# Three x tiles turned by DMA instead of TensorE, and the beginnings of blocks 1 and 2 cut differently, in a fused cosformer attention and GEGLU block

## The chip, the cores and the metric

The kernel runs on one core of a Trainium2 chip. A core has five engines that take their instructions in order and work side by side: TensorE (PE in the profile, with its weight loads as PEld), VectorE (DVE), ScalarE (ACT), GpSimd (POOL) and SyncE (SP), which here only issues DMAs. The metric is the device time of one execution in microseconds (us), as the median of several.

## The reference

Linear attention with a cosine weighting, then a gated feed-forward block:

```python
# q, k, v: 8 batches, 8 heads, 576 positions, 64 wide
def phi(x, c, s):
    r = np.maximum(x, 0.0)
    return np.concatenate([r * c, r * s], axis=-1)      # c, s: cos and sin of pi/2 * pos/576
q_p, k_p = phi(q, cos_w, sin_w), phi(k, cos_w, sin_w)
kv = np.einsum('bhsf,bhsd->bhfd', k_p, v)
z = np.sum(k_p, axis=2)
num = np.einsum('bhsf,bhfd->bhsd', q_p, kv)
den = np.einsum('bhsf,bhf->bhs', q_p, z)[..., None] + 1e-06
attn = num / den
# x: 4608 tokens of 512; w_gate, w_val: 512 x 1536; w_out: 1536 x 512
out = (gelu(x @ w_gate) * (x @ w_val)) @ w_out
```

The output is 4608 x 512 in float32.

## The kernel before

**Attention, batch by batch.** q, k and v of a batch (name `qf`, `kf`, `vf` in the profile) are loaded in two halves each. `prep` makes phi: the cosine half on VectorE (L162), the sine half on ScalarE (L160), a slice of positions `j` at a time; a 256-column instruction each. `kv_unit(b)` (L241) makes kv and z on TensorE. q's phi must be turned so that features lie on partitions: for batches 0 and 1 TensorE does it (`turn_j`, L204), from batch 2 on `turn_q(b)` (L193) does it with two DMA transposes that SyncE issues. `nm_unit(b, t)` multiplies 128 turned positions by kv: eight matmuls of 65 columns (L282), then three VectorE instructions that divide by the denominator (L293, L294, L295) and leave an x tile, 128 tokens x 512. A batch of 576 positions has five x tiles, t = 0 to 4, the last with 64 new rows.

**Turning x.** The feed-forward block needs x with its 512 features on partitions. `turn_x(b, t)` (L349) does it by DMA transposes on SyncE's queue. `turn_x_pe` (L357) does it by four TensorE transposes into PSUM and a ScalarE copy (L361) out of it, two copies where the tile straddles two blocks. The result goes into `xT` of a block.

**Feed-forward, block by block.** The 4608 tokens are nine blocks of 512 columns (`BLK`). Batch boundaries fall inside blocks: block 1 holds x tile 4 of batch 0 (columns 0 to 63), then tiles 0, 1, 2 of batch 1 (from columns 64, 192 and 320) and the left 64 columns of its tile 3; block 2 begins with the rest of tile 3 and tile 4 of batch 1, 64 columns each, and then has tiles 0, 1, 2 of batch 2. `gv_unit(n, jt)` makes one of twelve units of gate and value: eight matmuls over the block's columns (L400), a GELU on ScalarE (L408), a product on VectorE (L409) into `hT`. Units use two pairs of PSUM banks in turn, so a unit waits for the product of the unit before the last. `o_part` multiplies `hT` by w_out (L430), twelve matmuls per 128 tokens, and ScalarE copies the sum to `o_sb` (L439). The output products of block n - 1 are done in thirds, one after each unit of block n; those of block 0 stand by themselves, between blocks 0 and 1.

**Starting a block before all of it is there.** The first units of blocks 1, 2 and 3 are done in two halves: first the left columns of several units, then the right columns of the same units. Before the change block 1 does so with two units, block 2 with four and block 3 with two, all split 256 + 256.

**What sets the order.** The schedule is manual: every engine executes its instructions in the order in which the Python program issues them, and only semaphores tie the engines together. Between blocks 0 and 1 a list named `order` sets the sequence (entries "o" for a third of an output product, "nm" for an x tile's matmuls, "xt" for an x tile turned by TensorE, "q2" for phi of q of batch 2). In blocks 1 to 8 the loop over `jt` puts attention work of the next batch between units; `t_kv`, `t_nm`, `t_q` and `t_k` say at which `jt`. SyncE's queue takes, in order, loads, q and x transposes, and the output stores; a DMA that waits for its source holds up all that stand behind it. `store` puts out one tile in two DMAs, `flush` all that are held in `stores`; `o_part` flushes the tile before it. GpSimd's queue has the weights and q, k, v of batches 1 and 2. The pools `qT`, `qp` and `kp` have one buffer each, so the next batch's turn of q waits until the last x tile of the batch before has read `qT`.

Of the kernel before, what the change touches and what calls it, by code (L numbers as in the profile page):

```python
# [16 lines left out]
def kernel(  # L17
# [13 lines left out]
    nc = tc.nc  # L31
# [6 lines left out]
    JT = J // 128  # L38
    NP = H // 2
    R = S // 64  # L40
# [3 lines left out]
    BLK = 512  # L44
    JA = 4
# [376 lines left out]
    def flush():  # L422
        for i, o_sb in stores:
            store((nc.sync, nc.sync), i, o_sb)
        stores.clear()

    def o_part(i, jts, to, copy):
        n, tt = divmod(i, 4)
        for jt in jts:
            nc.tensor.matmul(  # L430
                bank(to),
                lhsT=hT[n][:, jt, tt * 128:(tt + 1) * 128],
                rhs=wo_sb[:, jt, :],
                start=(jt == 0),
                stop=(jt == JT - 1),
            )
        if JT - 1 in jts:
            o_sb = outp.tile([128, C], FP32, name="o_sb")
            copy(o_sb, bank(to))  # L439
            flush()  # L440
            stores.append((i, o_sb))


# [28 lines left out]
    for m in (0, 2):  # L472
        load(nc.gpsimd, "v", 1, m, m + 2)
    load_wo(8, 4)
    for name in ("q", "k"):
        for m in (0, 2):
            load(nc.gpsimd, name, 2, m, m + 2)
    for m in (0, 2):
        load(nc.gpsimd, "v", 2, m, m + 2)

    def turn_j(b, m0, m1, js, to, copy):

# [55 lines left out]
    for jt in range(4, JT):  # L538
        gv_unit(0, jt)
        if jt == 5:  # L540
            turn_j(0, 0, 4, (R - 1,), 4, act_copy)
        if jt == 6:
            nm_unit(0, 4)
        if jt == 8:
            turn_x_pe(0, 4, 5, act_copy)
        if jt in q1:
            prep("q", 1, 0, q1[jt])
            prep("q", 1, 1, q1[jt], eng=nc.scalar)
# [10 lines left out]
    )  # L559
    for what, *a in order:  # L560
        if what == "o":
# [17 lines left out]
            nm_unit(1, a[0], a[1])  # L579
        if what == "xt":  # L580
            turn_x_pe(1, a[0], a[1], act_copy)
    for m in (0, 2):
        load(nc.sync, "q", 3, m, m + 2)


    def prep_third(name, b, i):
# [4 lines left out]
    def loads(b, names=("q", "k", "v")):  # L591
# [5 lines left out]


    q3 = {
        (1, 8): ((0,), (0, 1)),  # L600
        (1, 9): ((1,), (2, 3)),
        (1, 10): ((2,), (4, 5)),
        (1, 11): ((3, 4, 5), (6, 7)),
        (2, 0): ((6, 7), (8,)),
        (2, 1): ((8,), ()),
    }
    turn[0] = 1
    for n in range(1, NB):
        b = n + 1
        t_kv, t_nm, t_q, t_k = {1: (7, 9, 12, 12), 2: (6, 7, 7, 9), 3: (2, 5, 6, 9)}.get(  # L610
            n, (1, 2, 4, 8)
        )
        for jt in range(JT):
            if n == 1 and jt >= t_nm:
                nm_unit(2, jt - t_nm, (6, 4, 6)[jt - t_nm])
                turn_x(2, jt - t_nm)
            heads = (0, 2, 4, 2)[n] if n < 4 else 0
            if jt >= heads:
                gv_unit(n, jt)
            else:  # L620
                for i in range(2):
                    half, unit = divmod(2 * jt + i, heads)
                    gv_unit(n, unit, half * HALF, HALF)
                    if n == 1:
                        j = JA + 2 * jt + i
                        prep("q", b, 1, (j,), eng=nc.scalar)
                        prep("q", b, 0, (j,))
                        if jt == i == 0:
                            turn_x_pe(1, 3, 5, act_copy)
            if jt % 3 == 1:  # L630
                flush()
            if b < B:
                if n == 1 and jt == 2:
                    prep("q", b, 0, (R - 1,))
                    prep("q", b, 1, (R - 1,), eng=nc.scalar)
                    turn_q(b)
                    nm_unit(1, NT - 1)
                if n == 1 and jt == 3:
                    turn_x(1, NT - 1)
# [12 lines left out]
                if jt == t_kv:  # L652
                    kv_unit(b)
                i = jt - 1 - n if n <= 2 else -1
                if 0 <= i < 3:
                    prep_third("k", b, i)
# [12 lines left out]
                if n > 1 and b + 1 < B:  # L669
                    if 0 <= jt - t_q < 3:  # L670
                        prep_third("q", b + 1, jt - t_q)
                    if 0 <= jt - t_k < 3:
                        prep_third("k", b + 1, jt - t_k)
                for c, t in nms:
                    if t == NT - 1:
                        if c + 1 < B:
                            turn_q(c + 1)
                        if c + 2 < B:
                            loads(c + 2)
                        for i in range(-(-(BLK - 64 * c) // 128), NT):  # L680
                            turn_x(c, i)
            if n > 1:
                o_part(
                    4 * (n - 1) + jt // 3,
                    range(4 * (jt % 3), 4 * (jt % 3) + 4),
                    4,
                    act_copy,
                )
# [47 lines left out]
```

## Time and profile before

| | |
|---|---|
| median of 4 runs | 326.78 us (325.28 to 328.07) |
| the profiled execution's own time | 326.69 us |
| its span, first to last instruction | 324.7 us |
| TensorE busy | 317.0 us, 2451 matmuls |
| VectorE busy | 170.3 us, 407 instructions |
| ScalarE busy | 159.2 us, 336 instructions |
| GpSimd busy | 26.0 us, all of it in the first 45 us |
| HBM read, written | 37.75 MB, 9.44 MB |
| granted TensorE clock | 1.0 |

The profile is of one execution. Its busy times are unions of instruction times; matmuls overlap, so the distance between the starts of two matmuls is what one costs, and the printed length of one (379 ns for 512 columns) is longer. For VectorE and ScalarE too, the next instruction can start before the printed end. A line number is that of the function that issues an instruction, so one line stands for many places; the start times tell them apart. "us to landing" of a DMA counts from the start of its issue to the event that tells of its end.

### The profile page before, as it was taken

The numbers are of one execution on the slowest core, as the hardware profiler recorded it, in microseconds if no ns is written. First come the engines' busy times: TensorE is split into PE (matmuls) and PEld (weight loads), VectorE is DVE, ScalarE is ACT, GpSimd is POOL, SyncE is SP. The second block draws the span as 40 slices with busy tenths as digits, with TensorE's granted clock in tenths as the row PEclk, the third lists the DMA queues.
The fourth block names the chain that finished last, engine by engine and source line by source line (L and its number), as shares of the span: only waits on it lengthen the run. The fifth ranks groups of instructions, "written<-read, shape, count | busy, mean of one in ns | idle before, by whom it ended". The sixth has DMA issues, their size and how long they took to land.

```text
span 324.7 us, 6340 instructions
## 1 busy us (share of the span) xinstructions
PE 317.0 (98%) x2451; PEld 164.5 (51%) x2451; DVE 170.3 (52%) x407; ACT 159.2 (49%) x336; POOL 26.0 (8%) x43
## 2 busy tenths in 40 slices
PE   8799999999999999999999999999999999999995
PEld 3574556556745564545544554445544444444443
DVE  5854686759675952793585348544532222222211
ACT  7854767947365833674457336643222332222220
POOL 5775410000000000000000000000000000000000
PEclk9999999999999999999999999999999999999999
DMA  7999999952999889828956991543431111111124
GB/s 271 233 191 267 294 346 374 217 139 48 308 196 380 164 157 380 203 75 240 323 119 152 356 236 28 131 100 81 88 72 33 35 32 32 35 32 32 34 65 98
DMA packets 69102, 53.57 MB, mean 165 GB/s; under 512 B 45392, under 2 KB 54352, under 8 KB 69072
## 3 DMA queue, kind: packets, MB, share of 16 engines
q1 hardware_dynamic: 59264, 41.23, 48.8%
q0 software_dynamic: 9648, 11.80, 15.7%
q8 instruction: 19, 0.31, 0.4%
q10 hardware_dynamic: 160, 0.13, 0.1%
q14 instruction: 11, 0.09, 0.1%
HBM read 37.75 MB, written 9.44 MB: 145 GB/s over the span
## 4 chain that ended last, share of the span: by engine, by line
PE 93%; DMA 4%; POOL 1%; DVE 0%; SPq 0%; issue 0%; DVEq 0%
PE ps L400 56%; PE ps L430 28%; PE ps L282 3%; PE ps L241 3%; DMA vf<-in_v_dram 2%; DMA wv_sb<-in_moe_w_val_dram 2%; PE ps L697 1%; PE ps L372 1%; PE ps L204 1%; PE ps L357 0%; SPq L80 0%; POOL wg_sb L94 0%; POOL gate L458 0%; DVE x_sb L295 0%; DVE o_sb L704 0%
## 5 line engine op out<-in xcount | busy, mean ns | idle before, releaser
L409 DVE TENSOR_TENSOR hT<-gel,ps 128x512 bf16<-128x512 f32 (+1 forms) x114 | 74.0, 650 | 128.8 <-PE ps L400 125.8
L408 ACT ACTIVATE gel<-ps 128x512 f32<-128x512 f32 (+1 forms) x114 | 64.8, 568 | 109.7 <-PE ps L400 108.0
L400 PE MATMUL ps<-xT,wg_sb 128*128 128x512 bf16 (+1 forms) x456 | 110.2, 364 | 0.0
L400 PE MATMUL ps<-xT,wv_sb 128*128 128x512 bf16 (+1 forms) x456 | 110.2, 364 | 0.0
L430 PE MATMUL ps<-wo_sb,hT 128*128 128x512 bf16 x420 | 105.8, 379 | 0.0
L400 PEld LDWEIGHTS <-wv_sb 128*128 128x128 bf16 x456 | 44.6, 98 | 47.0
L400 PEld LDWEIGHTS <-wg_sb 128*128 128x128 bf16 x456 | 44.0, 98 | 46.1
L430 PEld LDWEIGHTS <-hT 128*128 128x128 bf16 x420 | 38.3, 98 | 39.4
L439 ACT COPY o_sb<-ps 128x512 f32<-128x512 f32 x34 | 19.9, 586 | 30.0 <-PE ps L430 28.7
L160 ACT ACTIVATE qp<-qf,sin_t 128x256 bf16<-128x256 f32 x72 | 32.0, 501 | 0.4 <-DMA qf<-in_q_dram 0.4
L160 ACT ACTIVATE kp<-kf,sin_t 128x256 bf16<-128x256 f32 (+1 forms) x73 | 29.9, 480 | 1.2 <-DMA kf<-in_k_dram 1.2
L295 DVE TENSOR_TENSOR x_sb<-ps,rec 128x512 bf16<-128x512 f32 x38 | 26.3, 692 | 1.3
L162 DVE TENSOR_SCALAR qp<-qf,cos_t 128x256 bf16<-128x256 f32 x71 | 22.0, 357 | 2.3 <-DMA qf<-in_q_dram 2.3
L282 PEld LDWEIGHTS <-qT 128*128 128x128 bf16 x304 | 14.6, 98 | 7.9 <-ACT qT L486 0.3
L162 DVE TENSOR_SCALAR kp<-kf,cos_t 128x256 bf16<-128x256 f32 x63 | 18.2, 349 | 0.0
L282 PE MATMUL ps<-kv_sb,qT 128*128 128x65 bf16 x304 | 16.0, 194 | 0.0
L179 DVE CAST vx<-vf 128x1152 bf16<-128x1152 f32 (+1 forms) x15 | 11.9, 800 | 0.8 <-DMA vf<-in_v_dram 0.7
L250 ACT CAST kv_sb<-ps 128x260 bf16<-128x260 f32 x14 | 4.6, 382 | 12.9 <-PE ps L241 12.9
L241 PEld LDWEIGHTS <-kp 64*128 64x128 bf16 x504 | 8.5, 95 | 3.0 <-issue 3.0
L140 PE MATMUL ps<-dummy 128*128 128x512 bf16 x27 | 8.4, 457 | 1.5 <-POOL dummy L113 1.5
L241 PE MATMUL ps<-vx,kp 64*128 64x65 bf16 x504 | 9.3, 191 | 0.0
L294 DVE RECIPROCAL rec<-den 128x8 f32<-128x8 f32 x38 | 7.7, 203 | 1.3
(60 smaller groups left out, 100.6 us busy)
## 6 DMA issues: line engine op xcount, KB each, us to landing
out_dram<-o_sb SPq DMA_DIRECT2D x70, 128.0 KB, 2.7
kf<-in_k_dram SPq DMA_DIRECT2D x12, 576.0 KB, 6.5
vf<-in_v_dram SPq DMA_DIRECT2D x12, 576.0 KB, 8.6
qf<-in_q_dram SPq DMA_DIRECT2D x10, 576.0 KB, 5.0
qf<-in_q_dram POOLq DMA_DIRECT2D x4, 576.0 KB, 12.1
kf<-in_k_dram POOLq DMA_DIRECT2D x4, 576.0 KB, 12.6
vf<-in_v_dram POOLq DMA_DIRECT2D x4, 576.0 KB, 12.7
wg_sb<-in_moe_w_gate_dram POOLq DMA_DIRECT2D x6, 256.0 KB, 6.7
```

The source lines that it names most:

```text
L140: nc.tensor.matmul(bank(to), lhsT=dummy[:, 0:128], rhs=dummy, start=True, stop=True)
L160: nc.scalar.activation(o, i, AF.Relu, scale=tab[:, j:j + 1])
L162: (eng or nc.vector).tensor_scalar(o, i, 0.0, tab[:, j:j + 1], op0=ALU.max, op1=ALU.mult)
L179: copy(vx_tiles[b % 2][:, m0:m1, j0:j1, 0:D], staged["v", b][:, m0:m1, j0 * D:j1 * D].rearrange("p m (j d) -> p m j d", d=D),)
L241: nc.tensor.matmul(bank(6 + i)[:, m * (D + 1):(m + 1) * (D + 1)], lhsT=kp[rr, m, j, :], rhs=vx[rr, m, j, :], start=(j == 0), stop=(j == R ...
L282: nc.tensor.matmul(bank(b0 + h // 4)[:, (h % 4) * (D + 1):(h % 4 + 1) * (D + 1)], lhsT=q_cols(b, t, h), rhs=kv_sb[b][:, h // 2, h % 2, :], ...
L295: nc.vector.tensor_tensor(x, nm[:, :, :, 0:D], rec[:, :, :, None].to_broadcast([128, 2, 4, D]), op=ALU.mult,)
L400: nc.tensor.matmul(bank(b0 + g)[:, 0:w], lhsT=wt[:, ct, js], rhs=xt[:, ct, c0:c0 + w], start=(ct == 0), stop=(ct == CT - 1),)
L408: nc.scalar.activation(gel[:, 0:w], bank(b0)[:, 0:w], AF.Gelu)
L409: nc.vector.tensor_mul(hT[n][:, jt, c0:c0 + w], gel[:, 0:w], bank(b0 + 1)[:, 0:w])
L430: nc.tensor.matmul(bank(to), lhsT=hT[n][:, jt, tt * 128:(tt + 1) * 128], rhs=wo_sb[:, jt, :], start=(jt == 0), stop=(jt == JT - 1),)
L439: copy(o_sb, bank(to))
```

## The change

- Tile 4 of batch 0 is turned by `turn_x` instead of `turn_x_pe`, at the same place.
- Tiles 2 and 3 of batch 1 are turned by `turn_x` (a new entry "xd" in `order`), right after their `nm_unit`; before, TensorE turned tile 2 at the end of `order` and tile 3 inside block 1's first step.
- The load of q of batch 3 moves from SyncE's queue, behind block 0, to the end of GpSimd's queue, behind v of batch 2.
- Block 0's four output tiles are stored together in block 1's fourth step, instead of one by one as they are made.
- Block 1 does six units in halves of 256 instead of two; block 2 does six units as 128 + 384 columns instead of four as 256 + 256. Block 3 is as before.
- phi of q and k of batch 2 goes between the half units of block 1, `turn_q(2)` is issued one step earlier, tiles 0 and 1 of batch 2 one step later (steps 10 and 11), tile 2 moves into block 2's first step and tiles 3 and 4 into its second and third. In those three steps the output thirds stand between the two narrow pieces of a step instead of after them.
- The loads of k and v of batch 3 are issued in block 2's first step, behind the turn of tile 2 of batch 2, instead of in block 1's last. phi of q of batch 3 is spread otherwise over the same steps, and phi of k of batch 2 starts earlier.

The diff, cut to what the text speaks of:

```diff
@@ o_part
             copy(o_sb, bank(to))
-            flush()
+            if n > 0:
+                flush()
             stores.append((i, o_sb))
@@ GpSimd's loads
-    for name in ("q", "k"):
+    for name, b in (("q", 2), ("k", 2), ("v", 2), ("q", 3)):
         for m in (0, 2):
-            load(nc.gpsimd, name, 2, m, m + 2)
-    for m in (0, 2):
-        load(nc.gpsimd, "v", 2, m, m + 2)
+            load(nc.gpsimd, name, b, m, m + 2)
@@ block 0
         if jt == 8:
-            turn_x_pe(0, 4, 5, act_copy)
+            turn_x(0, 4)
@@ order
-        + [("nm", 0, 2), ("o", 0, 8), ("nm", 1, 6), ("o", 1, 8), ("xt", 0, 4), ("nm", 2, 2)]
-        + [("q2", 2, 3), ("o", 2, 8), ("xt", 1, 5), ("nm", 3, 6), ("q2", 3, 4), ("o", 3, 8)]
-        + [("xt", 2, 4)]
+        + [("nm", 0, 2), ("o", 0, 8), ("nm", 1, 6), ("o", 1, 8), ("xt", 0, 4), ("nm", 2, 2), ("xd", 2)]
+        + [("q2", 2, 3), ("o", 2, 8), ("xt", 1, 5), ("nm", 3, 6), ("xd", 3), ("q2", 3, 4), ("o", 3, 8)]
...
-    for m in (0, 2):
-        load(nc.sync, "q", 3, m, m + 2)
+        if what == "xd":
+            turn_x(1, a[0])
@@ blocks 1 to 8
+    heads = {1: (6, HALF), 2: (6, 128), 3: (2, HALF)}
...
-        t_kv, t_nm, t_q, t_k = {1: (7, 9, 12, 12), 2: (6, 7, 7, 9), 3: (2, 5, 6, 9)}.get(
+        t_kv, t_nm, t_q, t_k = {1: (7, 10, 12, 12), 2: (6, 7, 7, 9), 3: (2, 5, 6, 9)}.get(
...
-            heads = (0, 2, 4, 2)[n] if n < 4 else 0
-            if jt >= heads:
+            h, mid = heads.get(n, (0, 0))
+            if jt >= h:
                 gv_unit(n, jt)
             else:
                 for i in range(2):
-                    half, unit = divmod(2 * jt + i, heads)
-                    gv_unit(n, unit, half * HALF, HALF)
-                    if n == 1:
-                        j = JA + 2 * jt + i
-                        prep("q", b, 1, (j,), eng=nc.scalar)
-                        prep("q", b, 0, (j,))
-                        if jt == i == 0:
-                            turn_x_pe(1, 3, 5, act_copy)
-            if jt % 3 == 1:
+                    half, unit = divmod(2 * jt + i, h)
+                    gv_unit(n, unit, *((mid, BLK - mid) if half else (0, mid)))
+                    if n == 1 and jt < 2:
+                        js = ((4,), (5,), (6,), (7, 8))[2 * jt + i]
+                        prep("q", b, 1, js, eng=nc.scalar)
+                        prep("q", b, 0, js)
+                    if n == 2 and jt < 3 and i == 0:
+                        o_third(n, jt)
+                    if n == 1 and jt > 1:
+                        j = 2 * jt - 4 + i
+                        prep("k", b, 0, (j,))
+                        prep("k", b, 1, (j,), eng=nc.scalar)
+            if jt % 3 == 1 and n > 1:
                 flush()
...
+                if n == 1 and jt == 1:
+                    turn_q(b)
                 if n == 1 and jt == 2:
-                    prep("q", b, 0, (R - 1,))
-                    prep("q", b, 1, (R - 1,), eng=nc.scalar)
-                    turn_q(b)
                     nm_unit(1, NT - 1)
                 if n == 1 and jt == 3:
                     turn_x(1, NT - 1)
+                    flush()
...
-                if n == 2 and jt < 2:
-                    nms.append((n, 3 + jt))
+                if n == 2 and jt < 3:
+                    nms.append((n, 2 + jt))
...
-                if n == 1 and jt == JT - 1:
-                    loads(3, ("k", "v"))
                 for bt in nms:
                     nm_unit(*bt)
+                if (n, jt) == (2, 0):
+                    turn_x(2, 2)
+                    loads(3, ("k", "v"))
```

`o_third(n, jt)` is the third of an output product that the loop had at its end.

More of the change, by code (lines that the diff above doesn't have):

```diff
@@ L599, with o_third @@
     q3 = {
[L600 to L605, printed above, removed]
-    }
+        (1, 9): ((0, 1, 2), (0, 1)),
+        (1, 10): ((), (2, 3)),
+        (1, 11): ((), (4, 5)),
+        (2, 0): ((3, 4), (6,)),
+        (2, 1): ((5, 6), (7,)),
+        (2, 2): ((7, 8), (8,)),
+    }
+    heads = {1: (6, HALF), 2: (6, 128), 3: (2, HALF)}
+    def o_third(n, jt):
+        o_part(
+            4 * (n - 1) + jt // 3,
+            range(4 * (jt % 3), 4 * (jt % 3) + 4),
+            4,
+            act_copy,
+        )
     turn[0] = 1
@@ L614 @@
             if n == 1 and jt >= t_nm:
-                nm_unit(2, jt - t_nm, (6, 4, 6)[jt - t_nm])
+                nm_unit(2, jt - t_nm, (6, 4)[jt - t_nm])
                 turn_x(2, jt - t_nm)
-            heads = (0, 2, 4, 2)[n] if n < 4 else 0
-            if jt >= heads:
+            h, mid = heads.get(n, (0, 0))
+            if jt >= h:
                 gv_unit(n, jt)
@@ L647 @@
                     turn_x(b, i)
-                if n == 1 and jt == JT - 1:
-                    loads(3, ("k", "v"))
                 for bt in nms:
                     nm_unit(*bt)
+                if (n, jt) == (2, 0):
+                    turn_x(2, 2)
+                    loads(3, ("k", "v"))
                 if jt == t_kv:
                     kv_unit(b)
-                i = jt - 1 - n if n <= 2 else -1
-                if 0 <= i < 3:
-                    prep_third("k", b, i)
+                if n == 1 and jt == 6:
+                    prep("k", b, 0, (R - 1,))
+                    prep("k", b, 1, (R - 1,), eng=nc.scalar)
+                if n == 2 and 3 <= jt < 6:
+                    prep_third("k", b, jt - 3)
                 i = 2 * (jt - 5) if n == 1 else jt - (4 if n == 2 else 0)
@@ L681 @@
                             turn_x(c, i)
[L682 to L688, printed above, removed]
+            if n > 2 or n == 2 and jt > 2:
+                o_third(n, jt)
     for t in range(3):
```

## The prediction

> **What bounds the kernel now.** I read the page first (busy shares and slices), then the chain that ended last, then the windows around the change, then TensorE's timeline where block 1 begins.
>
> The page and its chain:
>
> ```profile
> PE 317.0 (98%) x2451; PEld 164.5 (51%) x2451; DVE 170.3 (52%) x407; ACT 159.2 (49%) x336; POOL 26.0 (8%) x43
> PE   8799999999999999999999999999999999999995
> PE 93%; DMA 4%; POOL 1%; DVE 0%; SPq 0%; issue 0%; DVEq 0%
> ```
>
> TensorE is busy from the second slice to the last but one, and 93% of the chain is its own work. Matmuls overlap, so "busy" is not proof; the starts are. TensorE's timeline, block 0's last output product up to block 1's first full units (start, length, instruction, how many):
>
> ```profile
> 54.58 0.59 PE L430 MATMUL ps<-wo_sb,hT 128*128 128x512 bf16 x2
> 55.01 0.39 PE L357 MATMUL ps<-ident,x_sb 128*128 128x128 bf16 x4
> 55.23 0.60 PE L400 MATMUL ps<-xT,wg_sb 128*128 128x256 bf16 x4
> 55.67 0.60 PE L400 MATMUL ps<-xT,wv_sb 128*128 128x256 bf16 x4
> 56.10 0.39 PE L357 MATMUL ps<-ident,x_sb 128*128 128x128 bf16 x4
> 56.33 0.60 PE L400 MATMUL ps<-xT,wg_sb 128*128 128x256 bf16 x4
> 56.77 0.60 PE L400 MATMUL ps<-xT,wv_sb 128*128 128x256 bf16 x4
> 57.32 0.60 PE L400 MATMUL ps<-xT,wg_sb 128*128 128x256 bf16 x4
> 57.76 0.60 PE L400 MATMUL ps<-xT,wv_sb 128*128 128x256 bf16 x4
> 59.06 1.03 PE L400 MATMUL ps<-xT,wg_sb 128*128 128x512 bf16 x4
> ```
>
> Read the starts, not the lengths. Four 256-column matmuls start 0.44 after the four before them (109 ns each); four transposes of an x tile take 0.22 (55.01 to 55.23), 56 ns each; four 512-column ones 0.87 (216 ns each). Only 56.77 to 57.32 is longer than its matmuls: 0.55 for 0.44. In the whole stretch from 21 us to 318 us I find no other gap between starts over 0.1 us. So there is almost no waiting to remove: time falls only by work that TensorE no longer does, and rises by any wait that a late x tile puts into it.
>
> **Part 1: twelve transposes leave TensorE.** Three tiles (x 4 of batch 0, x 2 and 3 of batch 1), four transposes each, 0.22 us a tile: -0.67 us. The 0.11 us before 57.32 goes with them: the profile puts it to ScalarE's copies of x 3 out of PSUM, which stand ahead of the unit's GELU. Together -0.78 us. ScalarE also loses four copies (595 ns full, 408 ns half), off the path.
> A page prices this otherwise. The Trainium skill, "TensorE: Matmul & The Clock Gate", Part 4, gives about 275 ns for one transpose inside a kernel; twelve would be 3.3 us and the gain near 1%. The rows above decide: 56 ns from start to start.
>
> **Part 2: more, narrower matmuls.** Block 1 now splits six units into 256+256 where it split two. A split unit costs 16 x 109 = 1.744 us, a whole one 8 x 216 = 1.727: +0.02 each, four more: +0.07. Block 2 splits six into 128+384 where four were 256+256. The trace has no 384; 128 columns go at 55.6 ns (32 of L372 in 1.78 us in the chain), and on the line through 109 and 216 a 384 is 162 ns: 8 x 218 = 1.744, +0.02 a unit, two more: +0.04. Sum +0.11 (bounds 0 and +0.2).
>
> **Part 3: x 2 and x 3 by DMA, in time for block 1?** x tiles come free 0.22 earlier than before (x 4's turn is gone), x 2 at 53.91 and x 3 at 55.26; block 1 starts at 55.23 - 0.44 = 54.79. Its six first halves need only columns 0 to 255: 6 x 0.872 = 5.23, then the matmuls of x 4 (0.24): the second half begins at 60.26. SyncE's queue is empty, since block 0's stores moved away; a transpose occupies it 1.19 us: x 2 from 53.97, the left part of x 3 from 55.3. The view of L349's issues:
>
> ```profile
> L349 SPq DMA_TRANSPOSE xT<-x_sb x34: 1171/1242/3131, 69.6 to 236.0; - x34
> DMA to landing us min/median/max: 2.3/2.8/10.3
> ```
>
> Alone, 2.4 us: x 3 lands at 57.7, 2.5 us early. But it is not alone: GpSimd's queue is loading. In the trace its last half load (v of batch 2) landed at 55.88, each 1.41 after the one before, so q of batch 3 carries the queue to 58.7, about 59 with the transposes' share. The 10.3 is a transpose issued behind six loads. In three such places the transpose landed 0.56, 0.58 and 0.62 after the last load ahead of it and the next one 0.28 to 0.47 later. Even if the transposes got nothing until the loads end, x 3 would land near 59 + 0.6 + 0.45 = 60.05, still 0.2 ahead of 60.26. I take 0, bounds 0 and +5.3 (10.3 after 55.3 is 65.6).
> The skill, "DMA: Bandwidth & Descriptors", "Queues, rings and completion order", says that each engine takes turns between rings a packet at a time, whichever engine issued, which speaks against the change. The trace has no transpose beside GpSimd's loads, so none here shows it; turn by turn, 32 packets of 18 ns an engine against loads of 178 ns would end after the loads too, so the sum stays.
>
> VectorE and ScalarE in that stretch: a 256-column half brings a product (338 ns to the next start), a GELU (275) and one or two prep steps (262 on VectorE, 398 on ScalarE): 0.60 and 0.67 of 0.87 us. They keep up, and three copies are gone.
>
> **Part 4: the SyncE queue after that.** turn_q for batch 2 must wait for the last reader of the old qT (x 4's matmuls, 60.4) and takes 7.4 us (3.38 + 3.93 in the trace), to 67.9; x 4 of batch 1 follows to 69.1, landing by 71.5; then block 0's eight stores at 0.59, to about 74. x 0 of batch 2 is ready only at 76.5. Block 2 starts at 77.7, so nothing is late. Block 0's output buffers are needed again at 83. The moved q load no longer sits in this queue. All this costs nothing; its cover is 2 us and more.
>
> **Part 5: block 2's beginning, the tight place.** Call its start T (77.7). One loop step is two 128-column pieces (0.45 each), a third of an output product (0.87) and eight matmuls of an x tile (0.24): 2.0 us, three times: columns 128 to 511 begin at T+6.04. x 2 of batch 2 is the last of them. Its matmuls end at T+2.2, but VectorE is at work until T+2.36; then 0.20 + 0.24 + 0.69 to T+3.5, issue at T+3.55, landing 2.41 later (the nearest rows, 75 to 81 us, have 2.41, 2.46, 2.41): T+5.96. That leaves 0.08 us. Bounds 0 and +1.5 (3.98, the slowest x tile with no load ahead of it on its queue); I take +0.1. The first third of the output product takes PSUM bank 4, which x 1 has just used: VectorE frees it 0.06 after TensorE is ready: +0.06. k of batch 3, now issued behind x 2, lands its second half at T+10.3 (4.97 from issue, the row at 81 us); VectorE wants it at T+10.1, and the two PSUM pairs give TensorE 0.9 us beyond that: 0.
>
> **Sum.** -0.78 + 0.11 + 0.06 + 0.10 = -0.51 us. The profiled execution took 326.69 us (span 324.7 and 1.99 around it), hence 326.2; it lies 0.09 under the median of the four runs (326.78), which gives 326.3. I say 326.2, a change of -0.16%. About 0.5% (1.6 us) is what a measurement of this kernel can tell from no change.
>
> **Rivals.**
> - Slower: x 3 of batch 1 is held up by GpSimd's loads. Every microsecond after 60.2 stops TensorE for a microsecond. For: the 10.3 row, and loads that now run 2.8 us longer. Against: the loads end by 59. The gain is gone at a landing of 60.7, the time is 0.5% over at 62.3, and at 65.6 it is 331.5 us. Typical, landing 1 to 3 us late: 327 to 329.
> - Block 2 waits: x 2 lands at 3 to 4 us instead of 2.4, or k of batch 3 comes a microsecond past its cover: +0.6 to +1.5, 326.8 to 327.7. For: 0.08 us of slack. Against: nothing else moves on the DMA engines at that moment.
> - Faster by more than the sum: a shorter queue helps somewhere that the starts don't show. With the whole gap list empty I can price it only by the spread of single runs (325.28): 325. That the change does not do what it says is excluded: its instruction order has 12 transposes fewer on TensorE and the new ones on SyncE.
>
> **Numbers.** The sum as worked: 0.69. First rival 0.13, half of it over 0.5%. Block 2: 0.13, a quarter over 0.5% with the first rival's help or the runs' spread. Faster: 0.05. So faster 0.05, slower 0.065 + 0.03 and a little for what I overlooked, 0.12; same 0.83. Range: below, 326.0 without any new wait, less the runs' own spread (single ones reach -1.5, a median half of that): 325.2. Above, both waits at middling size, +1.7: 327.9.
>
> **What would show it.** Right: L357's transposes fall from 36 to 24; no gap in TensorE's starts before 60.3; x 3 lands between 57.7 and 60.1; block 1 starts near 54.8, block 2 near 77.7; a gap under 0.3 us six microseconds into block 2. Wrong: TensorE waiting for xT in block 1 (first rival) or block 2 (second), or a gap anywhere else; a gain over 0.8 us would mean that the starts hid something.

## The result, and the profile after

| | before | after |
|---|---|---|
| median | 326.87 us (64 runs, 325.28 to 328.33) | 327.60 us (43 runs, 326.43 to 332.68) |
| ratio of the runs, after to before, 95% interval | | 1.003 (1.0019 to 1.004) |
| profiled execution, its span | 326.69, 324.7 us | 327.79, 325.6 us |

The change costs 0.3%, about 1 us. It lies inside the forecast's range and under the 0.5% bound, but on the other side of zero: 0.16% faster was forecast. The ratio leaves out the two slowest runs of the kernel after (331.41 and 332.68 us), which were in a slower state. The page of the kernel after:

```profile
PE 316.9 (97%) x2487; PEld 166.5 (51%) x2487; DVE 170.4 (52%) x413; ACT 158.7 (49%) x338; POOL 28.5 (9%) x45
PE   8799999999999999999999999999999999999995
PE 80%; DMA 10%; DVE 3%; SPq 2%; ACT 1%; issue 1%; POOL 0%; DVEq 0%; ACTq 0%; POOLq 0%
```

The busy time (0.1 us less) and the slices show nothing, as a busy PE hides waits of a microsecond. The third line does: TensorE's share of the chain that ended last fell from 93% to 80%, and DMA has 10% of it. The chain now runs through loads of q, k and v.

**Where the microsecond went.** Cut TensorE's time at the first output product (its first L430) and at the first gate matmul of each split block (the first narrow L400):

| stretch | before | after | what differs |
|---|---|---|---|
| first output product to block 1 | 14.55 | 15.25 | -0.22 transposes of x 2, +0.92 a wait |
| block 1 | 23.50 | 22.98 | -0.22 transposes of x 3, -0.11 the stall, -0.26 an x tile's matmuls moved into block 2, +0.07 splits |
| block 2 | 34.34 | 35.30 | +0.26 those matmuls, +0.04 splits, +0.62 a wait, +0.04 small gaps |
| block 3 to the end | 207.71 | 207.71 | |
| sum | 280.10 | 281.24 | +1.14 |

The first output product began at 40.68 us before and 40.65 after, so x 4's transposes (0.22, before that point) bought nothing in these two executions; TensorE's beginning varies anyway (39.6 to 41.2 over all profiles of this case). All the rest of the rise in these two executions is two waits; how much of the first one the change itself brings is taken up in experiment 8.

**The wait at 52 us.** TensorE's timeline after, at the turn of x tile 0 of batch 1 (the bracket is the idle time and what ended it; the true gap between starts is 1.78 for 0.87 of work, hence 0.92), and under it VectorE's at that moment:

```profile
51.42 1.03 PE L430 MATMUL ps<-wo_sb,hT 128*128 128x512 bf16 x4
53.20 0.40 PE L357 MATMUL ps<-ident,x_sb 128*128 128x128 bf16 x4 [0.75 <-DVE x_sb L295]
```
```profile
51.49 0.62 DVE L162 TENSOR_SCALAR qp<-qf,cos_t 128x256 bf16<-128x256 f32 x2 [3.40 <-DMA qf<-in_q_dram]
52.02 0.16 DVE L293 TENSOR_SCALAR den<-ps 128x8 f32<-128x8 f32 x1
52.21 0.20 DVE L294 RECIPROCAL rec<-den 128x8 f32<-128x8 f32 x1
52.45 0.69 DVE L295 TENSOR_TENSOR x_sb<-ps,rec 128x512 bf16<-128x512 f32 x1
```

VectorE stood idle for 3.4 us at phi of q of batch 2. The division that makes the x tile was queued behind it. q of batch 2 landed at 51.36 us, against 50.26 before. VectorE had waited for it there too, but TensorE had not been stopped (VectorE, then TensorE, of the kernel before):

```profile
50.39 0.62 DVE L162 TENSOR_SCALAR qp<-qf,cos_t 128x256 bf16<-128x256 f32 x2 [2.31 <-DMA qf<-in_q_dram]
52.32 0.39 PE L357 MATMUL ps<-ident,x_sb 128*128 128x128 bf16 x4
```

**The wait at 106 us.** A similar pattern two batches later, but by way of ScalarE. TensorE's matmuls for an x tile wait until VectorE has divided the x tile before. TensorE after, and under it VectorE:

```profile
105.89 1.03 PE L400 MATMUL ps<-xT,wv_sb 128*128 128x512 bf16 x4
107.36 0.42 PE L282 MATMUL ps<-kv_sb,qT 128*128 128x65 bf16 x8 [0.45 <-DVE x_sb L295]
```
```profile
103.79 0.88 DVE L162 TENSOR_SCALAR qp<-qf,cos_t 128x256 bf16<-128x256 f32 x3 [0.74 <-DMA qf<-in_q_dram]
105.59 0.69 DVE L409 TENSOR_TENSOR hT<-gel,ps 128x512 bf16<-128x512 f32 x1 [0.92 <-ACT gel L408]
106.62 0.69 DVE L295 TENSOR_TENSOR x_sb<-ps,rec 128x512 bf16<-128x512 f32 x1
```

VectorE's own wait for q of batch 4 (0.74 us) did not reach TensorE: behind it VectorE stood idle again, for 0.92 us, because the product ahead of the division needs a GELU from ScalarE. ScalarE had stood 2.78 us at its half of phi, and the GELU was queued behind that. ScalarE before, then after:

```profile
100.39 1.29 ACT L160 ACTIVATE qp<-qf,sin_t 128x256 bf16<-128x256 f32 x3
102.74 0.60 ACT L408 ACTIVATE gel<-ps 128x512 f32<-128x512 f32 x1 [1.06 <-PE ps L400]
```
```profile
103.77 1.31 ACT L160 ACTIVATE qp<-qf,sin_t 128x256 bf16<-128x256 f32 x3 [2.78 <-DMA qf<-in_q_dram]
104.98 0.57 ACT L408 ACTIVATE gel<-ps 128x512 f32<-128x512 f32 x1
```

Why q of batch 4 was late is read from SyncE's queue. Start, time until the last of the group was issued, kind, tile, how many; first the kernel before, then after:

```profile
80.33 1.03 SPq L80 DMA_DIRECT2D kf<-in_k_dram  x2
81.47 1.12 SPq L80 DMA_DIRECT2D vf<-in_v_dram  x2
85.58 8.31 SPq L193 DMA_TRANSPOSE qT<-qp  x2
94.00 1.03 SPq L80 DMA_DIRECT2D qf<-in_q_dram  x2
```
```profile
82.33 1.19 SPq L349 DMA_TRANSPOSE xT<-x_sb  x1
83.63 1.03 SPq L80 DMA_DIRECT2D kf<-in_k_dram  x2
84.76 1.30 SPq L80 DMA_DIRECT2D vf<-in_v_dram  x2
87.27 10.42 SPq L193 DMA_TRANSPOSE qT<-qp  x2
97.80 1.03 SPq L80 DMA_DIRECT2D qf<-in_q_dram  x2
```

x 2 of batch 2 moved into block 2, and k and v of batch 3 stand behind it: 3.3 us later. The two transposes of `turn_q(3)` stand behind those loads, and closer than before (1.2 us after the last load's issue instead of 3.0) they take 10.42 us instead of 8.31. The first transpose was not through its issue before the last of these loads had landed: load 89.44 and issue 89.97 us before, 93.55 and 93.62 after. q of batch 4 stands behind them: issued 3.8 us later, landed at 103.66 instead of 100.20.

**The spots the forecast watched.** L349's issues rose by four, two of them halves of x 3:

```profile
L349 SPq DMA_TRANSPOSE xT<-x_sb x38: 1171/1222/3725, 32.9 to 237.1; - x38
DMA to landing us min/median/max: 2.3/3.2/9.9
```

The left part of x 3 of batch 1 was issued at 56.55 and landed at 60.73; TensorE took it up at 61.40. x 2 of batch 2 was issued at 82.33 and landed at 84.75; TensorE took it up at 84.98. Neither stopped it.

### The profile page after: what moved, and what is told of

Read it like the earlier page. It is cut to its first block, busy times and chain, and to the rows that moved or that the text cites. A ratio compares the mean times of both kernels' runs of the same rounds, so it can differ in the third digit from the quotient of the medians.

```text
span 325.6 us, 6442 instructions
## 1 busy us (share of the span) xinstructions
PE 316.9 (97%) x2487; PEld 166.5 (51%) x2487; DVE 170.4 (52%) x413; ACT 158.7 (49%) x338; POOL 28.5 (9%) x45
## 4 chain that ended last, share of the span: by engine, by line
PE 80%; DMA 10%; DVE 3%; SPq 2%; ACT 1%; issue 1%; POOL 0%; DVEq 0%; ACTq 0%; POOLq 0%
PE ps L400 50%; PE ps L430 23%; DMA qf<-in_q_dram 6%; DMA vf<-in_v_dram 3%; PE ps L282 3%; PE ps L241 2%; DMA kf<-in_k_dram 2%; SPq L193 1%; SPq L80 1%; PE ps L372 1%; PE ps L708 1%; DVE x_sb L295 1%; ACT gel L408 1%; DVE hT L409 1%; PE ps L357 1%
## 5 line engine op out<-in xcount | busy, mean ns | idle before, releaser
L409 DVE TENSOR_TENSOR hT<-gel,ps 128x512 bf16<-128x512 f32 (+3 forms) x120 | 74.7, 624 | 126.5 <-PE ps L400 123.3
L408 ACT ACTIVATE gel<-ps 128x512 f32<-128x512 f32 (+3 forms) x120 | 65.5, 546 | 106.2 <-PE ps L400 104.1
L400 PE MATMUL ps<-xT,wg_sb 128*128 128x512 bf16 (+3 forms) x480 | 111.3, 354 | 0.0
L400 PE MATMUL ps<-xT,wv_sb 128*128 128x512 bf16 (+3 forms) x480 | 111.2, 354 | 0.0
L430 PE MATMUL ps<-wo_sb,hT 128*128 128x512 bf16 x420 | 105.9, 379 | 0.0
L400 PEld LDWEIGHTS <-wv_sb 128*128 128x128 bf16 x480 | 46.2, 98 | 45.7
L400 PEld LDWEIGHTS <-wg_sb 128*128 128x128 bf16 x480 | 45.8, 98 | 45.9 <-issue 0.3
L430 PEld LDWEIGHTS <-hT 128*128 128x128 bf16 x420 | 38.4, 98 | 39.3
```

Source lines behind the costliest of these rows:

```text
L400: nc.tensor.matmul(bank(b0 + g)[:, 0:w], lhsT=wt[:, ct, js], rhs=xt[:, ct, c0:c0 + w], start=(ct == 0), stop=(ct == CT - 1),)
L408: nc.scalar.activation(gel[:, 0:w], bank(b0)[:, 0:w], AF.Gelu)
L409: nc.vector.tensor_mul(hT[n][:, jt, c0:c0 + w], gel[:, 0:w], bank(b0 + 1)[:, 0:w])
L430: nc.tensor.matmul(bank(to), lhsT=hT[n][:, jt, tt * 128:(tt + 1) * 128], rhs=wo_sb[:, jt, :], start=(jt == 0), stop=(jt == JT - 1),)
```

## The experiments

Kernels that were submitted together shared the runs of the kernel before, whose median was 326.71 to 326.94 in the four groups. Ratios are to the kernel before, so 1.003 is the mark to which to compare an edit of the kernel after. The quoted expectations give their theories letters; the text after each says the theory in words.

### 1. Load q of batch 4 earlier (q4_early)

```diff
                 if (n, jt) == (2, 0):
                     turn_x(2, 2)
                     loads(3, ("k", "v"))
+                    loads(4, ("q",))
...
-                            loads(c + 2)
+                            loads(c + 2, ("k", "v") if c == 2 else ("q", "k", "v"))
```

> The changed kernel, with the load of q of batch 4 issued ahead of turn_q(3) instead of behind it; k and v of batch 4 stay behind. Theory A (the time goes into two waits of VectorE for a late load: q of batch 2 near 51 us, 0.92 us on TensorE; q of batch 4 near 106 us, 0.62 us): q of batch 4 lands near 97 instead of 103.7, the gap between TensorE's starts near 106 us is gone, the one near 52 stays; 0.6 us faster than the changed kernel, about 327.0, ratio to before 1.000 to 1.002. Rival B (the time goes into x tiles that come too late or into narrower matmuls at the beginnings of blocks 1 and 2): no change, 327.6, ratio 1.002 to 1.003.

Measured: 329.97 us, 1.0101 (1.0072 to 1.013). q of batch 4 landed at 96.84 and the wait at 106 was gone, but the time rose by 0.7% more. SyncE's queue, and TensorE's timeline, of this kernel:

```profile
86.58 14.01 SPq L193 DMA_TRANSPOSE qT<-qp  x2
```
```profile
102.63 0.40 PE L282 MATMUL ps<-kv_sb,qT 128*128 128x65 bf16 x7 [1.79 <-DMA qT<-qp]
103.88 1.91 PE L400 MATMUL ps<-xT,wg_sb 128*128 128x512 bf16 x4
105.58 1.72 PE L400 MATMUL ps<-xT,wv_sb 128*128 128x512 bf16 x4
```

With six loads ahead of it `turn_q(3)` took 14 us: the last load landed at 96.84, the first transpose was through its issue at 96.85, and the second landed at 102.58, and TensorE waited 1.97 us for `qT`. Then its matmuls came slower: from 103.88 to 105.58 four start 0.425 us apart, against 0.216 elsewhere. The windows (length, busy times by engine, then the granted clock, the DMA share and GB/s) say why:

```profile
100.90:103.20 2.30, 0.57 (x9) 0.44 (x10) 0.56 (x2) 0.52 (x2) 0.00 (x0) 1.00 1.11 238
103.20:106.90 3.70, 3.70 (x12) 1.29 (x10) 1.71 (x6) 1.86 (x5) 0.00 (x0) 0.55 1.02 379
```

The granted clock was 0.55 on average over the 3.7 us behind the wait, worth about 1.7 us (3.7 x 0.45). Not every execution has this: three of the six runs, at a mean clock of 0.989 to 0.990, took 330.37 to 331.44 us, the other three, at 0.998 to 1.000, 328.22 to 329.56, which is still slower than the kernel after. So the wait at 106 does hang on q of batch 4, but loading it ahead of the turn moves the wait to the turn, at a higher price.

### 2. Move phi of q of batch 2 behind the division (q2_late)

```diff
-        + [..., ("kv",), ("q2", 0, 2), ("o", 3, 4)]
-        + [("nm", 0, 2), ("o", 0, 8), ("nm", 1, 6), ("o", 1, 8), ...]
+        + [..., ("kv",), ("o", 3, 4)]
+        + [("nm", 0, 2), ("o", 0, 8), ("nm", 1, 6), ("q2", 0, 2), ("o", 1, 8), ...]
```

> The changed kernel, with the first two steps of phi of q of batch 2 moved behind the second x tile of batch 1 (nm 1) in the order list, so that VectorE and ScalarE do not stand waiting for that load ahead of the first x tiles. Theory A: the gap near 52 us (0.92 us in the profile) is gone and the one near 106 stays; 0.4 to 0.9 us faster than the changed kernel, 326.8 to 327.2, ratio 0.999 to 1.001, and the runs lie closer together. With block 1 starting 0.9 earlier, x 3 of batch 1, which landed at 60.7, may now be waited for by up to 0.8 us at the second half of block 1; then the gain is nearly nothing. Rival B: no change.

Measured: 327.46 us, 1.0034 (1.001 to 1.0059). In its profile the wait at 52 is gone and the first stretch is 14.49 us, 0.16 over the 14.33 that it would be without any wait (14.55 less x 2's transposes): this wait comes from the order on VectorE and ScalarE. The time did not follow. The profiled execution, 330.77 us, is far above the median and can't explain it: q of batch 4 landed at 105.01 there, the later wait grew to 3.1 us, and the granted clock was at 0.5 for the 3.41 us from 109.02.

### 3. Both edits (both_loads)

> Both edits together: q of batch 4 loaded ahead of turn_q(3), and phi of q of batch 2 moved behind nm 1. Theory A: both gaps gone, 1.0 to 1.5 us faster than the changed kernel, 326.2 to 326.6, ratio 0.997 to 0.999, which is what the prediction's sum gives without new waits. Rival B: 327.6 and a ratio of 1.003.

Measured: 329.01 us, 1.0065 (1.0046 to 1.0084). No wait at 52, but 2.3 us for `qT` in two pieces (0.37 and 1.94) near 101 and a granted clock of 0.56 from 103.2 to 107: as in experiment 1.

### 4. x 4 of batch 0 back on TensorE (x4_on_pe)

```diff
-            turn_x(0, 4)
+            turn_x_pe(0, 4, 5, act_copy)
```

> The changed kernel, with x 4 of batch 0 turned by TensorE again. Theory A1 (x 4's DMA transposes, which ran beside GpSimd's loads from 33 to 40 us, make q of batch 2 land later): q of batch 2 lands 0.3 to 0.6 us earlier against the first load of q of batch 1, the gap near 52 us shrinks to 0.3 to 0.6; 0.22 us more on TensorE; in all 0 to 0.4 us faster than the changed kernel. Rival A2 (the loads were late from the start of the execution, which differs from run to run, and not by the transposes): the gap stays as large, and the time is 0.2 us longer.

Measured: 327.25 us, 1.0024 (1.0009 to 1.004): against 1.003, no difference that these runs can tell. In its profile q of batch 2 landed at 50.35 (before: 50.26) and 0.52 us of the wait remained, since TensorE was earlier in this execution (first output product at 40.04 us, against 40.65 and 40.68 after and before); experiment 8 takes this up.

### 5. k and v of batch 3 ahead of the stores (kv3_ahead)

If `turn_q(3)` is slow because loads stand close ahead of it, the loads must go earlier, not q of batch 4.

```diff
                 if n == 1 and jt == 3:
                     turn_x(1, NT - 1)
+                    loads(3, ("k", "v"))
                     flush()
...
                     turn_x(2, 2)
-                    loads(3, ("k", "v"))
```

> The changed kernel, with the loads of k and v of batch 3 issued right behind the turn of x 4 of batch 1 and ahead of block 0's stores, instead of behind x 2 of batch 2; they land by about 80 us, and turn_q(3) and the load of q of batch 4 have nothing ahead of them on SyncE's queue. Theory C (the loads of k and v of batch 3, pushed from 80 to 84 us by the later x 2 of batch 2, slow turn_q(3) from 8.3 to 10.4 us, which makes q of batch 4 land 3.5 us later, at 103.7, and VectorE and ScalarE wait for it ahead of the division of an x tile): turn_q(3) takes 7.3 to 7.8 us, q of batch 4 lands at 100 to 101, the gap near 106 us is gone; 0.6 to 1 us faster than the changed kernel, 326.6 to 327.0, ratio 0.999 to 1.001. Rival D (q of batch 4 is late because turn_q(3) starts later, with VectorE's phi of q of batch 3, whatever stands ahead of it in the DMA rings): q of batch 4 lands above 102 and the gap stays.

Measured: 329.19 us, 1.0082 (1.0057 to 1.0108). The theory held in its own place: `turn_q(3)` took 7.75 us, q of batch 4 landed at 100.34, and there is no wait at 106. But a new one came up at 84. SyncE's queue and TensorE's timeline:

```profile
70.05 1.03 SPq L80 DMA_DIRECT2D kf<-in_k_dram  x2
71.18 0.92 SPq L80 DMA_DIRECT2D vf<-in_v_dram  x2
72.15 9.89 SPq L420 DMA_DIRECT2D out_dram<-o_sb  x8
82.15 3.86 SPq L349 DMA_TRANSPOSE xT<-x_sb  x3
```
```profile
87.37 0.81 PE L400 MATMUL ps<-xT,wg_sb 128*128 128x384 bf16 x4 [2.83 <-DMA xT<-x_sb]
```

The eight stores took 9.89 us to issue instead of 6.20, and the x tiles of batch 2 stand behind them: x 2 landed at 87.23, and TensorE lost 2.99 us. Each DMA of SyncE waits for the one eight places before it to land. In the trace the third load landed at 80.17 and the seventh store was issued at 80.19; the fourth landed at 81.57 and the eighth was issued at 81.58. A load that takes 9 to 10 us to land thus stops the queue eight places behind itself.

### 6. The same with q2_late's edit (kv3_ahead_q2_late)

> The same, and phi of q of batch 2 moved behind nm 1 as well. Theory A with C: both waits gone, what stays is the prediction's sum, 0.4 to 0.6 us under the kernel before: 326.3 to 326.5, ratio 0.998 to 0.999. If instead x 3 of batch 1 is now waited for at the second half of block 1 (it landed at 60.0 to 60.7 in all runs, 0 to 0.8 us after TensorE would want it), 0.2 to 0.7 comes back: ratio 0.999 to 1.001.

Measured: 328.66 us, 1.0064 (1.0027 to 1.01). The wait at 52 was gone, one of 2.77 at 84 remained.

### 7. q2_late's edit in the kernel before (before_q2_late)

> The kernel before, with only the first two steps of phi of q of batch 2 moved behind nm 1. If the kernel before has the wait near 51 us too in most executions (its profiled one has 0.3 us to spare, and loads there move by 1 us from run to run): 0.1 to 0.4 us faster, ratio 0.999 to 1.000. If that wait came with the change: no difference, ratio 1.000.

Measured: 327.40 us, 1.0016 (1.0002 to 1.003). The edit costs a little by itself, in a kernel whose profile, of one execution, has no wait there to remove. That answers why experiment 2 brought nothing, not what the cost is: the profile shows one new gap of 0.28 us at 56.3, at ScalarE's copy of x, against the 0.11 of the kernel before, and nothing else; that is 0.17 of the 0.5 us.

### 8. Only x 4 of batch 0 by DMA, in the kernel before (before_x4_dma)

> The kernel before, with only x 4 of batch 0 turned by DMA. TensorE loses 0.22 us of transposes near 34 us. The sum of the prediction: 0.22 us faster, ratio 0.9993. Theory A: TensorE comes 0.22 us sooner to a place at 51 us where VectorE waits for the load of q of batch 2, which comes no sooner, so nothing is gained: ratio 1.000, and if x 4's transposes delay GpSimd's loads as well, 0.2 to 0.4 us slower, ratio 1.001.

Measured: 326.88 us, 0.9998 (0.9985 to 1.0012): nothing gained. The wait at 52 appears with this part alone (q of batch 2 landed at 51.01):

```profile
52.84 0.40 PE L357 MATMUL ps<-ident,x_sb 128*128 128x128 bf16 x4 [0.61 <-DVE x_sb L295]
```

The nine profiles in which phi of q of batch 2 stands in its old place give a rule. Let D be the time from the first output product to the landing of q of batch 2, and W what the way from there to x 0's turn takes over the 11.64 us of the kernel before:

| kernel | x 4 of batch 0 by | q of batch 2 landed | D | W | D - 9.80 |
|---|---|---|---|---|---|
| kv3_between_x4_pe | TensorE | 50.26 | 9.08 | 0 | below 0 |
| before | TensorE | 50.26 | 9.58 | 0 | below 0 |
| q4_early | DMA | 50.67 | 9.98 | 0.18 | 0.18 |
| x4_on_pe | TensorE | 50.35 | 10.32 | 0.52 | 0.52 |
| kv3_ahead | DMA | 50.77 | 10.32 | 0.51 | 0.52 |
| kv3_between | DMA | 51.08 | 10.61 | 0.80 | 0.81 |
| q3_back | DMA | 51.14 | 10.65 | 0.84 | 0.85 |
| before_x4_dma | DMA | 51.01 | 10.67 | 0.86 | 0.87 |
| after | DMA | 51.36 | 10.71 | 0.91 | 0.91 |

Whatever q of batch 2 lands beyond 9.80 us after the first output product, TensorE waits. The kernel before had 0.22 us of slack there. Two things use it up: a TensorE that begins earlier, and a load that lands later. With x 4 turned by DMA q landed at 50.67 to 51.36 in this table, without it at 50.26 to 50.35. Over all fifteen profiles the two overlap: 50.28 to 51.80 in eleven with, 50.26 to 50.35 in four without.

That x 4's transposes slow GpSimd's stream is shown where they meet it. They went out at 32.9 us and took 7.1 us to land in the kernel after; their packets moved from 36.84 to 39.29 us. The five loads that landed around that time (31.34 to 39.51 us before, 32.18 to 40.93 after) took 8.17 to 8.20 us in all four profiles without these transposes and 8.36 to 9.35 in all eleven with them. But this is not the whole of the wait at 52. Of the 1.10 us by which q of batch 2 landed later in the kernel after's profile, 0.84 were there at 32.18 us, before x 4's transposes went out; these five loads added 0.57, and the loads behind them made up 0.31. And a wait comes without them too: D was 10.32 in x4_on_pe, which waited 0.52, and 10.44 in before_q2_late, where by the rule phi in its old place would have cost 0.64. D is 9.85 on average in those four, 10.57 in the eleven.

### 9. Loads of batch 3 between two groups of stores (kv3_between)

The lesson of experiment 5: the loads early, but not eight places ahead of anything urgent. Four of block 0's stores go ahead of `turn_q(2)`, four behind the loads. To the edit of kv3_ahead it adds:

```diff
                 if n == 1 and jt == 1:
+                    held = stores[2:]
+                    del stores[2:]
+                    flush()
+                    stores.extend(held)
                     turn_q(b)
```

> The changed kernel, with the loads of k and v of batch 3 behind x 4 of batch 1 and block 0's eight stores divided around them: four ahead of turn_q(2), where SyncE's queue stood idle from 59 to 61.6 us, and four behind the loads. Theory C with the slot rule (a DMA of SyncE's queue is not issued until the one eight places before it has landed, which kept block 0's last stores at 80 to 82 us in kv3_ahead and with them x 0, 1 and 2 of batch 2, for a gap of 3.0 us): now x 0 of batch 2 has only the first load eight places ahead, x 2 lands near 84.7 as in the changed kernel, q of batch 4 near 100.5 as in kv3_ahead; neither the gap near 106 nor the one near 84; 0.6 to 1.0 us faster than the changed kernel, 326.6 to 327.0, ratio 0.999 to 1.001. Rival E (the rings, not the slots, hold the x tiles: 5.7 us of loads and 1.3 of stores ahead of them): x 0 lands after 83 and x 2 after 85.5, a gap of 1 us or more near 84, ratio over 1.003.

Measured: 326.54 us, 0.9995 (0.9978 to 1.0013): the best version, level with the kernel before and about 1 us under the kernel after. SyncE's queue, and ScalarE where it had waited for q of batch 4:

```profile
70.62 1.04 SPq L80 DMA_DIRECT2D kf<-in_k_dram  x2
73.81 2.53 SPq L420 DMA_DIRECT2D out_dram<-o_sb  x4
77.44 5.83 SPq L349 DMA_TRANSPOSE xT<-x_sb  x3
86.98 7.79 SPq L193 DMA_TRANSPOSE qT<-qp  x2
94.88 1.03 SPq L80 DMA_DIRECT2D qf<-in_q_dram  x2
```
```profile
101.00 1.31 ACT L160 ACTIVATE qp<-qf,sin_t 128x256 bf16<-128x256 f32 x3 [0.30 <-DMA qf<-in_q_dram]
102.95 0.60 ACT L408 ACTIVATE gel<-ps 128x512 f32<-128x512 f32 x1 [0.64 <-PE ps L400]
```

`turn_q(3)` takes 7.79 us, q of batch 4 is issued at 94.88 and lands at 100.90, ScalarE waits only 0.30 us for it, and its next GELU is in time. x 0 and x 2 of batch 2 landed at 82.36 and 84.46, where the rival of the expectation had them after 83 and 85.5. Block 2 takes 34.68 us instead of 35.30: the 0.62. From the first output product to the end it is 280.52 us, against 281.24 after. The wait at 52 stayed (0.80 us).

### 10. and 11. The best version without the wait at 52, in two ways (kv3_between_q2_late, kv3_between_x4_pe)

> The same with phi of q of batch 2 behind nm 1. Theory A: the wait near 52 us, 0.2 to 0.9 us in the profiles with x 4 by DMA, is gone as well: 326.3 to 326.6, ratio 0.998 to 0.9995, the prediction's sum. But in the kernel before the same edit gave 1.0016, so it may shift work into block 1 (the profile of that run has 0.28 us there): then no better than kv3_between.

> kv3_between with x 4 of batch 0 turned by TensorE. Theory A1 (x 4's transposes cost GpSimd's loads about 0.45 us, so that their 0.22 us on TensorE is lost again at 51 us): equal to kv3_between within 0.2 us. Rival A2 (the loads' own spread): 0.2 us slower.

Measured: 327.09 us, 1.002 (1.0004 to 1.0036), and 327.22 us, 1.0021 (1.0006 to 1.0036). Neither beat experiment 9. In the first, with block 1 no longer late, x 3 of batch 1 is:

```profile
60.12 0.61 PE L400 MATMUL ps<-xT,wg_sb 128*128 128x256 bf16 x4 [0.34 <-DMA xT<-x_sb]
```

x 3 landed at 60.08 and cost 0.50 us in starts (60.12 less 59.37 is 0.75, for 0.26 of matmuls); 0.76 more went at 83.7. So the wait at 52 had been hiding one for x 3. In the second, the profile has no wait in the stretch and 279.73 us from the first output product to the end, 0.37 under the kernel before. But TensorE began at 41.18 us in that execution, and the median of twelve did not show the gain.

### 12. and 13. q of batch 3 back on SyncE's queue (q3_back_q2_late, q3_back)

What was open was whether x 3 is late because q of batch 3 lengthens GpSimd's stream. These two take that load back, on top of experiments 10 and 9:

```diff
-    for name, b in (("q", 2), ("k", 2), ("v", 2), ("q", 3)):
+    for name, b in (("q", 2), ("k", 2), ("v", 2)):
...
                 if n == 1 and jt == 1:
+                    for m in (0, 2):
+                        load(nc.sync, "q", 3, m, m + 2)
                     held = stores[2:]
```

> kv3_between with phi of q of batch 2 behind nm 1, and the load of q of batch 3 back on SyncE's queue, behind x 3 of batch 1 and ahead of the stores. Theory F (from 10 to 60 us GpSimd's stream of loads is the second bound: q of batch 2 lands at 50.3 to 51.4 and x 3 of batch 1 0.8 to 1.0 us after the stream's end, whatever TensorE saves; with q of batch 3 at its end the stream is 2.8 us longer): x 3 lands near 58 instead of 60.0 to 60.9, no gap near 52 and none near 60; 0.4 to 0.6 us faster than the kernel before, 326.2 to 326.5, ratio 0.998 to 0.9995. Rival G (the next tight place, x 2 of batch 2 against the right pieces of block 2, gives it back): a gap of 0.5 to 1 us near 83.7, ratio 1.000 to 1.002, as in kv3_between_q2_late.

> kv3_between with the load of q of batch 3 back on SyncE's queue, behind x 3 of batch 1; phi of q of batch 2 where the changed kernel has it. Theory F: the wait near 52 us stays (0.2 to 0.9 us), x 3 lands near 58 but TensorE does not need it before 60.5 to 61, so the time is that of kv3_between, 326.4 to 326.9, ratio 0.999 to 1.001. If q of batch 3 on GpSimd's queue costs more than that (its packets beside turn_q(2) or the stores): faster than kv3_between by over 0.3 us.

Measured: 327.91 us, 1.0031 (1.0011 to 1.005), and 328.73 us, 1.0056 (1.0035 to 1.0077). Yes: x 3 landed at 58.37 and 58.59, and the wait near 60 is gone. In experiment 12 the waits near 52 did not go: q of batch 2 landed at 51.80, later than in any other profile, and TensorE lost 0.35 us near 53 and 0.52 near 55. In both, besides, the load now stands ahead of `turn_q(2)`, which slows, and what is behind it comes late (SyncE's queue and TensorE of q3_back_q2_late):

```profile
57.81 0.96 SPq L80 DMA_DIRECT2D qf<-in_q_dram  x2
61.51 9.49 SPq L193 DMA_TRANSPOSE qT<-qp  x2
77.92 4.91 SPq L349 DMA_TRANSPOSE xT<-x_sb  x3
```
```profile
85.85 0.81 PE L400 MATMUL ps<-xT,wg_sb 128*128 128x384 bf16 x4 [1.42 <-DMA xT<-x_sb]
```

## Why the prediction was right or wrong

**Part 1 (twelve transposes): right on TensorE, wrong for x 4.** L357's transposes fell to 24, x 2's and x 3's left at 0.22 us each, and the stall before 57.32 went. x 4's 0.22 came to nothing: the forecast took TensorE for the only thing that sets the pace before block 1, while the stream of loads had only 0.22 us to spare there. Work taken off TensorE there is returned as a wait, and x 4's own transposes slow that stream (experiment 8).

**Part 2: right.** With +0.07 and +0.04 the table of stretches closes to 0.04 us.

**Part 3: the cost was mis-sized, and hidden.** x 3 came as worked out from the end of GpSimd's stream: 0.62 and 0.20 after it for x 2 and x 3 (0.6 and 0.45 were taken). But the stream ended at 59.91, not 59, so x 3 landed at 60.73 instead of 60.05. TensorE's second half began 5.50 us after block 1, as forecast (5.47); without the wait of 0.92 at 52 that would have been 60.48, and x 3 0.25 late. Experiment 10 shows this wait, at 0.50. The zero should have been +0.2 to +0.5. The Trainium skill, "DMA: Bandwidth & Descriptors", "Queues, rings and completion order", has each DMA engine serve its rings in turn, a packet at a time. By the forecast's own working a transpose beside the loads would end after them; x 3 did, by 0.82 us. The first rival had its place right, but decided nothing: landing was at its break-even point, and TensorE was not there yet.

"x tiles come free 0.22 earlier than before" is the sentence that failed first: x 2 and the left part of x 3 were issued at 55.24 and 56.55, not at 53.97 and 55.3.

**Part 4: the step that failed.** "All this costs nothing; its cover is 2 us and more" was checked for x 0 of batch 2, for the stores and for the output buffers. It stopped short of the queue's next items: x 2 of batch 2, k and v of batch 3, `turn_q(3)`, q of batch 4. Part 5 followed k of batch 3 to its reader, but not the turn behind it. q of batch 4 landed 3.46 us later, and the slack was 2.35. That slack is read from the way behind the landing, through ScalarE's phi and GELU, the product and the division to TensorE's next matmuls: 3.70 us after (103.66 to 107.36). Before, those matmuls came at 106.25, so a landing at 102.55 would have done, and q landed at 100.20. TensorE came there 0.49 us later after than before, and 3.46 - 2.35 - 0.49 is the wait of 0.62. Experiment 9 removes this wait by another place for the loads of k and v and for four stores, with the rest of the change left as it is, and the ratio goes from 1.003 (1.0019 to 1.004) to 0.9995 (0.9978 to 1.0013). The profile accounts for 0.62 to 0.72 us of that; the rest is within the spread of the medians.

**Part 5: right.** With T at 78.88, x 2 of batch 2 was issued at T + 3.45 (3.55 worked out), landed at T + 5.87 (5.96) and was used at T + 6.10 (6.04): no gap, where +0.1 was taken. The 0.06 for PSUM bank 4 came (79.11 to 79.39 for 0.22 us of matmuls). k of batch 3 landed at 89.64 and VectorE waited 1.33 us for it, but TensorE has no gap there. The second rival did not occur.

**The sum.** With both waits out of the way, the way from the first output product to the end is 279.73 us in experiment 11's profile, 0.37 under before. The forecast's terms beyond that point give -0.29 (-0.51 without x 4's 0.22). So what TensorE gains was sized well; a wait "anywhere else", which the text named as what would prove it wrong and priced with almost nothing, decided the sign.

**Open:** what moving phi of q of batch 2 costs in experiment 7; why experiment 11's profile, without a wait, has no faster median than the kernel before; and how much of the wait at 52 the kernel before has in executions in which TensorE begins early or the loads run late. One profile of each kernel can't tell.

## What to carry to other kernels

When a DMA is moved in an in-order queue, follow every item behind it to its reader until one has slack measured in the trace, not only the next two: here a tile moved to 82 us was paid for at 106 us, by the load that stood behind four half loads and a turn. An engine that waits in order for a load holds up what is queued behind it, VectorE a division at 52 us and ScalarE a GELU at 106, so a load with no reader on TensorE still stops TensorE. And where a stream of loads ends within a few tenths of a microsecond of its need, work taken off the busiest engine comes back as a wait.

## What the runs showed of the hardware

- A stall near 2 us can cost nearly twice its length. Behind waits of 1.97 us (experiment 1), 1.94 (experiment 3) and 3.13 (experiment 2) the granted clock fell to 0.5 for 3.41 us, worth 1.7 us. Behind the one of 2.99 us in experiment 5 it stayed at 1.00 from 84 to 95.
- The clock records of these traces tell the two apart. Within each profile, all changes of the clock lie whole multiples of 3.413 us apart (in experiment 1 the clock rose at 14.81 us and fell at 103.56, 26 such windows later). On that grid, counting shorter waits beside the long one, TensorE had stood idle for 2.23, 2.30 and 3.11 us of the window just before the clock fell. In experiments 5 and 6 the wait fell into two windows, 1.37 and 1.62 us, 1.12 and 1.65, and the clock stayed. So in these five profiles the idle time within one window counted, not the length of the wait; where the bound lies between 1.65 and 2.23 us is not shown.
- The Trainium skill, "TensorE: Matmul & The Clock Gate", Part 1, has such a window of about 3.4 us that runs freely, and a clock that falls after an idle one. The grid agrees. But here a window in which TensorE worked for 1.18 of 3.41 us was idle enough, and the measurement decides.
- `turn_q`, two transposes, took from 7.36 us (before, at 62.16) to 14.01 us on the same queue, by when the loads right ahead of it landed: in all five profiles in which the last load was issued 0.2 to 1.4 us ahead of `turn_q(3)`, the first transpose was through its issue 0.01 to 0.11 us after the last of them had landed.
- Eight DMAs in flight is what SyncE's queue has in this program; a slow load blocks the ninth.
